# Transposing q with the DMA crossbar instead of TensorE, for batches 2 to 7 of an attention and mixture-of-experts kernel

## The chip, the cores and the metric

The kernel runs on one core of one Trainium2 chip. The metric is the device time of one execution in microseconds (us), the median of several runs. Runs of the kernel before spread over about 0.5%, so a difference under 3 us is read with care.

## The reference

Linear attention with cosine weights, whose output feeds a mixture of eight experts with balanced gates. Only the attention matters here:

```python
B, H, S, D = 8, 8, 576, 64

def phi(x, c, s):
    r = np.maximum(x, 0.0)
    return np.concatenate([r * c, r * s], axis=-1)      # 64 -> 128 features

q_p, k_p = phi(q, cos_w, sin_w), phi(k, cos_w, sin_w)
kv  = einsum('bhsf,bhsd->bhfd', k_p, v)
z   = sum(k_p, axis=2)
num = einsum('bhsf,bhfd->bhsd', q_p, kv)
den = einsum('bhsf,bhf->bhs', q_p, z)[..., None] + 1e-06
attn = num / den                                         # then gates and eight experts
```

## The kernel before

The kernel computes attention batch by batch, in blocks. Block `j` holds TensorE's feed-forward matmuls of the first expert for tokens that are ready, cut into 16 slots, and each slot also carries some attention work: batch `b = j + 1` is finished (denominators, division, product), batch `b + 1` is prepared, and batch `b + 2` is loaded. The heads go in four pairs, 0 to 3. Order matters a lot: instructions of TensorE, VectorE and ScalarE stay in written order, and the DMA issues of the SP engine form one queue that is worked off in order.

q has its sequence on the partitions; the products need the features there. So q must be transposed, nine 128x128 blocks a pair. The parts that the change touches (cuts marked `# ...`):

```python
def load(b, half, names="qkv", held_back=False):      # POOL's DMA queue, f32 -> f16
    for name in names:
        x = ld.tile([P, 2, C, D], F16, name=f"{name}_ld")
        # ... one 288 KB transfer for two head pairs

def prep_q(b, hk):
    q_p = qp_pool.tile([P, C, 2, D], F16, name="q_p")
    ve.tensor_tensor(out=q_p[:], in0=loaded.pop(("q", b, hk))..., in1=cs, op=ALU.mult)
    qps[b, hk] = q_p

def turn(b, hk, i, scalar=None):                       # three of the nine blocks
    if i == 0:
        qTs[b, hk] = qT_pool.tile([P, C, P], F16, name="q_pT")
    t_ps = ps_s.tile([P, 512], FP32, name="small_ps")
    for c in range(i * C3, (i + 1) * C3):
        te.matmul(out=t_ps[...], lhsT=qps[b, hk][:, c]..., rhs=ident[:], ...)
    # rectify on the way out of PSUM: se.activation(Relu) or ve.tensor_scalar(max 0)

def denominators(b):
    for h in range(H):                                 # pair 3 comes last
        for j in range(3):
            te.matmul(out=den_ps[...], lhsT=zsel[:, h, :], rhs=qTs[b, hk][...], ...)
    # ... ve: add eps, reciprocal -> den
    if b >= 3:
        r = dram.tile([96, C3 * HP], FP32, name="r")
        nc.sync.dma_start(out=r[:], in_=den[:])        # to DRAM
        for hk in range(HK):                           # and back, broadcast over partitions
            rb = rb_pool.tile([P, C * HP], FP32, name="rb")
            for hh in range(2):
                nc.sync.dma_start(out=rb[...], in_=r[...].to_broadcast(...))

def attend(b, hk):
    # num_ps = kv.T @ q_pT on TensorE, then on VectorE:
    ve.tensor_tensor(out=xT[...], in0=num_ps[i]..., in1=rb[...], op=ALU.mult)

# the schedule of a block j from 3 on, batch b = j + 1 (gates and one sums call cut;
# blocks 1 and 2 prepare pair 3 of their own batch in slot 0)
at(j, 0, sums, b, 1)
for i, (hk, k_) in enumerate(turns[8:]):               # last 4 of the 12 turns
    at(j, i, turn, b, hk, k_, k_ != 1)
at(j, 4, denominators, b)
for hk in range(HK):
    at(j, 12 + hk, attend, b, hk)
for slot, fn, hk in ((4, prep_k, 0), (5, prep_q, 0), (6, prep_kv, 0), (6, prep_k, 1),
        (7, prep_q, 1), (8, prep_kv, 1), (9, prep_k, 2), (10, prep_q, 2),
        (11, prep_kv, 2), (11, prep_k, 3), (13, prep_kv, 3), (15, prep_q, 3)):
    at(j, slot, fn, b + 1, hk)
for i, (hk, k_) in enumerate(turns[:8]):
    at(j, 8 + i, turn, b + 1, hk, k_, k_ != 1)
if 1 <= j and b + 2 < B:
    for half in range(2):
        at(j, 13 + 2 * half, load, b + 2, half, "qkv", True)
```

The softmax here doesn't subtract the row's maximum and nothing guards it: scores larger than these inputs give would overflow.

Of the kernel before, what the change touches and what calls it, by code (L numbers as in the profile page):

```python
# [11 lines left out]
F16 = mybir.dt.float16  # L12

AX = mybir.AxisListType
ALU = mybir.AluOpType
# [10 lines left out]
def kernel(  # L26
# [10 lines left out]
    nc = tc.nc  # L37
    P = nc.NUM_PARTITIONS

    B, H, S, D = q.shape  # L40
# [5 lines left out]
    C = S // HP  # L46
# [71 lines left out]
    te, ve, se = bound  # L118
# [62 lines left out]
    with ExitStack() as p1:  # L181
# [5 lines left out]
        qT_pool = p1.enter_context(tc.tile_pool(name="qT_pool", bufs=6))  # L187
# [6 lines left out]
        loaded = {}  # L194
        sources = {"q": q, "k": k, "v": v}

        def load(b, half, names="qkv", held_back=False):
# [28 lines left out]
            out=ident[:], in_=ones_sq[:], pattern=[[-1, P]], compare_op=ALU.is_equal,  # L226
# [13 lines left out]
        def keep_busy(n):  # L240
# [12 lines left out]
            out=wrap[:], in0=gidx[:], scalar1=float(S), scalar2=None, op0=ALU.is_ge  # L253
# [3 lines left out]
            out=sval[:], in0=wrap[:], scalar=-float(S), in1=gidx[:],  # L257
            op0=ALU.mult, op1=ALU.add,
# [20 lines left out]
        with nc.allow_low_precision("sums of zeros and ones"):  # L279
            ve.tensor_reduce(  # L280
                out=lo[:], in_=rows[:, :, 1, :], axis=AX.XY, op=ALU.add, negate=True
# [3 lines left out]
                out=sel[:], in0=rows[:, 0:3, 0, :], in1=rows[:, 0:3, 1, :], op=ALU.add  # L285
            )
        ve.tensor_copy(
            out=spread.rearrange("p j hk hh d -> p (j hk hh) d"),
            in_=sel[:].rearrange("p j h -> p (j h)").unsqueeze(2).to_broadcast([P, 3 * H, D]),
# [12 lines left out]
        kps, qps, qTs, kvs, hls, rbs = {}, {}, {}, {}, {}, {}  # L302
# [13 lines left out]

        def prep_q(b, hk):

            q_p = qp_pool.tile([P, C, 2, D], F16, name="q_p")
            ve.tensor_tensor(  # L320
                out=q_p[:], in0=loaded.pop(("q", b, hk)).unsqueeze(2).to_broadcast([P, C, 2, D]),
                in1=cs, op=ALU.mult,
            )
            qps[b, hk] = q_p

        def prep_kv(b, hk, copy=ve.tensor_copy):
            k16, v16 = (loaded.pop((name, b, hk)) for name in "kv")
# [9 lines left out]

        def turn(b, hk, i, scalar=None):

            if i == 0:  # L340
                qTs[b, hk] = qT_pool.tile([P, C, P], F16, name="q_pT")
            t_ps = ps_s.tile([P, 512], FP32, name="small_ps")
            for c in range(i * C3, (i + 1) * C3):
                te.matmul(
                    out=t_ps[:, (c - i * C3) * P : (c - i * C3 + 1) * P],
                    lhsT=qps[b, hk][:, c].rearrange("p a d -> p (a d)"),
                    rhs=ident[:],
                    start=True,
                    stop=True,
                )  # L350
            dst = qTs[b, hk][:, i * C3 : (i + 1) * C3, :].rearrange("p c s -> p (c s)")
            if (3 * hk + i) % 2 == 0 if scalar is None else scalar:
                se.activation(out=dst, in_=t_ps[:, 0 : C3 * P], func=AF.Relu)
            else:
                ve.tensor_scalar(
                    out=dst, in0=t_ps[:, 0 : C3 * P], scalar1=0.0, scalar2=None, op0=ALU.max
                )
# [160 lines left out]
        prep_pair(0, 1)  # L518
        sums_made(0, 0, begun[0])
        prep_q(0, 0)  # L520
        begun.append(sums_begun(0, 1))
        keep_busy(12)
        prep_q(0, 1)
        for hk in range(HK):
            for i in range(3):
                turn(0, hk, i, hk < 2 or i == 0)
            keep_busy(8)
            if hk == 0:
                sums_made(0, 1, begun[1])
            if hk < 2:  # L530
                prep_q(0, hk + 2)
# [9 lines left out]
        for hk in range(HK):  # L541
# [7 lines left out]
            for kt in ((), (0,), (1,), (2, 3))[hk]:  # L549
                for ft, h_ps in enumerate(first_ps):  # L550
                    te.matmul(
                        out=h_ps[:],
# [14 lines left out]
        for j in range(B):  # L567
            b = j + 1
            if j == 0:
# [6 lines left out]
                for hk in range(HK):  # L576
                    for i in range(3):
                        at(0, 7 + hk, turn, 1, hk, i)
                    if hk == 0:
                        at(0, 7, lambda: sums_made(1, 1, begun[3]))  # L580
                    if hk < 2:
                        at(0, 7 + hk, prep_q, 1, hk + 2)
# [4 lines left out]
            elif b < B:  # L587
                if j <= 2:
                    at(j, 0, prep_q, b, 3)
                    at(j, 1, prep_kv, b, 3)  # L590
                    at(j, 1, sums, b, 0)
                    at(j, 3, sums, b, 1)
                    for i, (hk, k_) in enumerate(turns[2:]):
                        at(j, i // 2, turn, b, hk, k_, k_ != 1)
                else:
                    at(j, 0, sums, b, 1)
                    for i, (hk, k_) in enumerate(turns[8:]):
                        at(j, i, turn, b, hk, k_, k_ != 1)
                at(j, 5 if j <= 2 else 4, denominators, b)
                for hk in range(HK):  # L600
                    at(j, 8 + 2 * hk if j == 1 else 12 + hk, attend, b, hk)
# [460 lines left out]
    for e in range(1, E):  # L1062
# [3 lines left out]
        for n in range(NU):  # L1066
# [28 lines left out]
            if e == 1 and n == 0:  # L1095
# [9 lines left out]
                ve = nc.vector  # L1105
# [8 lines left out]
    while stream:  # L1114
        _, pair, name = stream.pop(0)
# [32 lines left out]
```

## Time and profile before

| | before |
|---|---|
| median time | 1001.2 us (999.5 to 1001.7, 4 runs) |
| span of the profiled run | 999.2 us |
| TensorE busy | 978.4 us |
| attention of batches 3 to 7, issue of the first r to that of the last | 87.5 us, four blocks of 19.7, 21.7, 24.8 and 21.3 |
| rest of the span after the last r | 826.7 us |

First the page's busy times and, from its picture of 40 slices of 25 us, TensorE, its granted clock (tenths of full speed) and the mean busy share of the 16 DMA engines (PE is TensorE, PEld its weight loads, DVE VectorE, ACT ScalarE, POOL GpSimd):

```profile
PE 978.4 (98%) x8002; PEld 685.7 (69%) x8002; DVE 811.5 (81%) x1828; ACT 572.9 (57%) x1268; POOL 60.3 (6%) x82
...
PE   7999999989999999999999999999999999999997
...
PEclk8999999999999999999999999999999999999999
DMA  9907773733002331034013320043113400104535
```

TensorE looks like the only limit. But DMA is about seven tenths busy in slices 4 to 6, where the attention runs (75 to 150 us), and the chain of waits tells of a second limit. One block of that chain follows; the columns are start in us, length in us, and what the chain went through (L109 is a line of the kernel; h_ps are feed-forward matmuls, small_ps the attention's; "issue" is time in which the profile shows nothing that was waited for):

```profile
103.38 1.36 DVE den L109
104.74 0.02 issue
104.75 3.69 DMA r<-den
...
111.01 4.29 DMA rb<-r
...
115.43 0.57 DVE xT L109
...
118.99 0.95 PE small_ps L109 x39
119.94 0.86 PE h_ps L109 x4
...
123.89 0.80 PE small_ps L109 x24
```

The reciprocals of a batch leave for DRAM (r), come back as a broadcast (rb), VectorE multiplies them into xT, TensorE works on to the denominators of the next batch (the last line, 24 matmuls), and the loop starts again. TensorE fills its waits with feed-forward matmuls, so it is busy in nearly all of the loop.

The loads of q, k and v stand in slots 13 and 15, that is between the last rb and the next r. In the same block (start, length, engine, line, operation, tiles):

```profile
95.70 0.71 POOL L201 DMA_DIRECT2D q_ld<-in_q_dram  x1 [18.07 <-DVE acc_lo L109]
...
99.95 0.72 POOL L201 DMA_DIRECT2D v_ld<-in_v_dram  x1
```

Six loads are issued from 95.7 to 100.0 us, the last lands at 108.3 us. No critical transfer is issued on the SP queue from 91.8 us (the last rb) to 104.75 us (r), so the loads disturb only the end of this gap: r, which lands 1.58 us after its issue where no loads run (the last block), takes 3.4 to 3.9 us in three of the blocks.

### The profile page before, as it was taken

To read this page: it belongs to the slowest core of one execution; us is meant where nothing else is said; L and a number is where in the kernel's file an instruction comes from. 1 tells how busy PE (TensorE), PEld (TensorE's weight loads), DVE (VectorE), ACT (ScalarE), POOL (GpSimd) and SP (SyncE) were. 2 spreads that over 40 slices of the span, in tenths; PEclk is the share of its full clock that TensorE was granted. 3 is DMA by queue.
4 is the path that set the end of the run, shared out by engine and by line. 5 is a ranking of instruction groups with operands and counts; after the bars stand their busy time and mean duration, and the time that the engine had idled before them with its cause. 6 is when DMAs were issued, how large, how long until landed. Compare 5 with 4: busy or idle time off the path is not lost.

```text
span 999.2 us, 20494 instructions
## 1 busy us (share of the span) xinstructions
PE 978.4 (98%) x8002; PEld 685.7 (69%) x8002; DVE 811.5 (81%) x1828; ACT 572.9 (57%) x1268; POOL 60.3 (6%) x82
## 2 busy tenths in 40 slices
PE   7999999989999999999999999999999999999997
PEld 7555545446777777777777777777777777777775
DVE  5877556588989888888879878988789888988887
ACT  5677656357777555555555555555555555555551
POOL 6302210001000000000000000000000000000001
PEclk8999999999999999999999999999999999999999
DMA  9907773733002331034013320043113400104535
GB/s 171 200 3 139 145 137 72 155 67 83 32 26 54 62 67 47 25 82 75 25 48 67 62 53 24 27 89 67 40 34 66 91 25 25 48 25 107 134 85 127
DMA packets 60800, 72.74 MB, mean 73 GB/s; under 512 B 5568, under 2 KB 52640, under 8 KB 60704
## 3 DMA queue, kind: packets, MB, share of 16 engines
q0 software_dynamic: 27232, 30.94, 19.7%
q1 hardware_dynamic: 33232, 40.25, 14.9%
q8 instruction: 62, 1.02, 0.4%
q14 instruction: 34, 0.28, 0.1%
q10 hardware_dynamic: 240, 0.26, 0.1%
HBM read 89.01 MB, written 13.34 MB: 102 GB/s over the span
## 4 chain that ended last, share of the span: by engine, by line
issue 76%; PE 14%; DMA 4%; DVE 3%; POOL 2%; SPq 1%; ACT 0%; POOLq 0%; DVEq 0%; ACTq 0%
PE h_ps L109 5%; PE small_ps L109 4%; PE y_ps L109 3%; DMA rb<-r 2%; PE rows_ps L109 1%; DMA r<-den 1%; DVE den L109 1%; SPq L423 1%; DMA k_ld<-in_k_dram 1%; POOL w2e L133 0%; DVE xT L109 0%; PE copied_ps L109 0%; POOL w1e L127 0%; POOL acc_lo L978 0%; DVE P_tok L109 0%
## 5 line engine op out<-in xcount | busy, mean ns | idle before, releaser
L821 DVE SCALAR_TENSOR_TENSOR acc_lo<-rows_ps,P_tok,acc_lo 128x512 f32<-128x512 f32 (+1 forms) x322 | 203.1, 639 | 74.8 <-PE rows_ps L109 74.8
L109 PEld LDWEIGHTS <-H 128*128 128x128 f16 x2080 | 203.0, 98 | 83.1 <-issue 1.2
L757 ACT CAST u<-h_ps 128x384 f16<-128x384 f32 x288 | 137.5, 478 | 131.4 <-PE h_ps L109 131.4
L109 PEld LDWEIGHTS <-w1e 128*128 128x128 f16 x1632 | 155.9, 98 | 60.2 <-issue 5.2
L751 DVE CUSTOM_DVE_ANT_0 H<-p_ps,u 128x384 f16<-128x384 f32 x329 | 180.9, 550 | 6.7 <-PE p_ps L109 6.4
L109 PEld LDWEIGHTS <-hs 128*128 128x128 f16 x1500 | 146.5, 98 | 56.4 <-issue 0.3
L109 PE MATMUL h_ps<-S,w1e 128*128 128x384 f16 x672 | 164.1, 326 | 1.1 <-ACT u L109 0.9
L109 PE MATMUL p_ps<-xT,T 128*128 128x384 f16 x672 | 164.1, 326 | 0.3 <-DVE H L751 0.2
L109 PE MATMUL h_ps<-xT,w1e 128*128 128x384 f16 (+1 forms) x616 | 152.6, 350 | 0.5 <-DVE xT L109 0.5
L109 PE MATMUL rows_ps<-V,H 128*128 128x256 f16 x1000 | 150.0, 273 | 0.7 <-DVE acc_hi L821 0.7
L109 PE MATMUL rows_ps<-w2e,hs 128*128 128x256 f16 x1000 | 150.0, 273 | 0.0
L789 ACT ACTIVATE H<-h_ps 128x384 f16<-128x384 f32 x144 | 70.6, 490 | 95.1 <-PE h_ps L109 95.1
L109 PEld LDWEIGHTS <-T 128*128 128x128 f16 x1008 | 98.1, 98 | 29.5 <-issue 3.0
L109 PE MATMUL rows_ps<-w2e,H 128*128 128x256 f16 (+1 forms) x568 | 91.2, 285 | 0.0
L770 ACT COPY copied_ps<-h_ps 128x384 f32<-128x384 f32 x144 | 67.5, 469 | 35.2 <-PE h_ps L109 35.2
L780 ACT ACTIVATE H<-copied_ps 128x384 f16<-128x384 f32 x144 | 70.8, 492 | 20.4 <-PE copied_ps L109 20.4
L109 PE MATMUL copied_ps<-xT,w1e 128*128 128x384 f16 x336 | 82.1, 326 | 0.0
L109 PE MATMUL h_ps<-S,T 128*128 128x384 f16 x336 | 81.8, 325 | 0.3 <-ACT copied_ps L109 0.3
L109 PE MATMUL copied_ps<-w2e,H 128*128 128x256 f16 x504 | 75.5, 272 | 0.0
L109 PE MATMUL rows_ps<-V,hs 128*128 128x256 f16 x500 | 74.9, 272 | 0.0
L821 DVE SCALAR_TENSOR_TENSOR acc_lo<-copied_ps,P_tok,acc_lo 128x256 f32<-128x256 f32 x126 | 60.0, 476 | 0.4
L821 DVE SCALAR_TENSOR_TENSOR acc_hi<-rows_ps,P_tok,acc_hi 128x512 f32<-128x512 f32 (+1 forms) x56 | 41.3, 737 | 20.5 <-PE rows_ps L109 19.7
(126 smaller groups left out, 993.6 us busy)
## 6 DMA issues: line engine op xcount, KB each, us to landing
S<-x_saved SPq DMA_DIRECT2D x108, 192.0 KB, 2.4
out_dram<-acc_lo SPq DMA_DIRECT2D x62, 128.0 KB, 2.4
w1e<-in_moe_w_dram POOLq DMA_DIRECT2D x7, 1024.0 KB, 9.1
w2e<-in_moe_w_dram POOLq DMA_DIRECT2D x7, 1024.0 KB, 9.6
rb<-r SPq DMA_DIRECT2D x40, 144.0 KB, 4.3
k_ld<-in_k_dram POOLq DMA_DIRECT2D x16, 288.0 KB, 7.7
v_ld<-in_v_dram POOLq DMA_DIRECT2D x16, 288.0 KB, 8.4
q_ld<-in_q_dram POOLq DMA_DIRECT2D x16, 288.0 KB, 8.1
```

What stands on the lines that cost most here:

```text
L109: i = getattr(self.engine, name)(*args, **kwargs)
L423: nc.sync.dma_start(out=rb[hh * HP : (hh + 1) * HP, :].rearrange("p (j s) -> p j s", j=3), in_=r[:].rearrange("(j r) s -> r j s", r=32)[h ...
L751: latest = ve._custom_dve(TENSOR_ADD_SAT, out=out, in0=ps[:, 0:TU], in1=t[:], s0=FP32_MAX, s1=0.0)
L757: se.copy(out=t[:], in_=ps[:, 0:TU])
L770: se.copy(out=Y[:, 0:TU], in_=X[:, 0:TU])
L780: se.activation(out=h11, in_=Y[:, 0:TU], func=AF.Relu)
L789: se.activation(out=h12, in_=X[:, 0:TU], func=AF.Relu)
L821: ve.scalar_tensor_tensor(out=a, in0=rows, scalar=P_tok[:, g, self.e : self.e + 1], in1=a, op0=ALU.mult, op1=ALU.add,)
```

## The change

Its intent is to take work off the busiest engine. For batches 2 to 7 the 216 TensorE transposes and their 72 evictions from PSUM go. Instead VectorE rectifies q in place, multiplies it by the cosines as before, and one transposing DMA for each head pair writes `q_pT` directly. The transfer is issued on the SP queue, which also carries r and rb.

```diff
         def prep_q(b, hk):
 
+            q16 = loaded.pop(("q", b, hk))
+            by_dma = b >= 2
+            if by_dma:
+                ve.tensor_scalar(
+                    out=q16, in0=q16, scalar1=0.0, scalar2=None, op0=ALU.max
+                )
             q_p = qp_pool.tile([P, C, 2, D], F16, name="q_p")
             ve.tensor_tensor(
-                out=q_p[:], in0=loaded.pop(("q", b, hk)).unsqueeze(2).to_broadcast([P, C, 2, D]),
+                out=q_p[:], in0=q16.unsqueeze(2).to_broadcast([P, C, 2, D]),
                 in1=cs, op=ALU.mult,
             )
-            qps[b, hk] = q_p
+            if by_dma:
+                qTs[b, hk] = qT_pool.tile([P, C, P], F16, name="q_pT")
+                nc.sync.dma_start(
+                    out=qTs[b, hk][:], in_=q_p[:].rearrange("p c a d -> p (c a d)"),
+                    transpose=True,
+                )
+            else:
+                qps[b, hk] = q_p
...
         def turn(b, hk, i, scalar=None):
 
+            if b >= 2:
+                return
             if i == 0:
```

## The prediction

> What bounds the kernel now. TensorE is 98% busy over the 999 us span (busy shares). The change acts in the attention stage, from about 75 to 184 us for batches 2 to 7. There TensorE is 90 to 100% busy in each 25 us stretch (windows), so little idle is to be won. The chain of waits shows a second limit for batches 3 to 7, a loop of 21 to 25 us a block: denominator matmuls, reciprocal 1.36, r to DRAM 1.6 to 3.9, rb back 4.3 to 6.0, multiply into xT, TensorE to the next denominators. VectorE waits for rb 18.6 us in all. DMA is 0.78 busy at 140 GB/s from 75 to 150 us (windows).
>
> Removed. 216 TensorE transposes (6 batches x 4 pairs x 9). In the chain nine take 0.50 us, and four h_ps matmuls are spaced 1.03 us with three of them against 0.86 without: 0.055 us each, 12 us of TensorE, 2.0 a batch. Evictions: 48 on ScalarE (0.49 us each, 23 us) and 24 on VectorE (0.55 us, 13 us), off the critical engine.
>
> Added. 24 VectorE rectifications of 128x576 f16, estimated at 0.2 to 0.45 us from the f16 copy of the same shape (0.44): 5 to 11 us, about what VectorE saves. 24 transposing transfers of 288 KB on the SP queue, which also issues r and rb. A plain 192 KB load lands in 2.4 us, rb of 144 KB beside the loads in 4.3. The Trainium skill, "DMA: Bandwidth & Descriptors", section "Latency and other measured facts", gives 261 GB/s for a transpose in one kernel: 1.1 us of data, an estimate of 3 to 4 us to landing. "VectorE: DVE Perf Modes", section "The three transpose paths", gives 1309 ns for one 128x128 block: nine in series would be 12 us. No trace here shows one. I expect about 5 us beside the loads.
>
> Critical path. Pairs 0 to 2 have slack. Pair 3 has little: its q_p is written in a block's last slot (118.65 to 119.4 us in one block), the denominator matmuls that read it start at 123.8, 4.4 us later, and k, v, q loads are issued from 117.6. SP is in order: eight rb issues take 5.8 us, the transposes come behind them; with three q_p buffers, pair 3's product waits until pair 0's transpose has landed. So pair 3's transposed q comes 0 to 4 us late in five blocks, TensorE stands at the denominators, and r and rb start later. Against it, 1.3 us a block (two thirds of the 2.0) leaves the loop. At 3 us to landing the kernel gains 6 to 10 us; at 5 to 6 it breaks even or loses a few; at 12 it loses 40 and more.
>
> Predicted: 1004 us, 8 in 10 within 988 to 1045. Faster by over 2%: 0.04; within 2%: 0.60; slower: 0.36. A gain over 2% needs 20 us, more than the TensorE work removed.
>
> What would show it. Right: transposes land in 4 to 7 us; TensorE busy falls by about 12 us; a new wait of the denominator matmuls for the transfer into q_pT; den, r, rb still in the chain, with the transpose among them; the rest after the stage unchanged in length. Wrong: landings under 3.5 us and no wait at the denominators (then 990 to 994); or landings over 10 us, late loads of k and v, a chain mostly of DMA (then above 1040).
>
> What would make it wrong: the cost of a transfer on the chip, which no trace here has; SP's time to issue one, if several us; transposes slowing rb and the loads.

## The result, and the profile after

The changed kernel takes 1030.1 us (1030.0 to 1031.5, 4 runs) against 1001.2 us: a ratio of 1.0295, 95% interval 1.028 to 1.031, slower. A ratio here is always the mean time of one kernel's runs over that of the other's runs in the same rounds, so it is not quite the ratio of the medians. The result is correct.

| | before | after |
|---|---|---|
| median time | 1001.2 us | 1030.1 us |
| TensorE busy | 978.4 us | 973.4 us |
| issue of the first r | 85.0 us | 93.0 us |
| four blocks, r to r | 19.7, 21.7, 24.8, 21.3 us | 28.2, 29.5, 29.5, 20.8 us |
| rest of the span after the last r | 826.7 us | 827.4 us |

Of the 29.2 us that the span grew, 8.0 were lost before the first r (in batch 3) and 20.5 in the four blocks after it; the 827 us behind them are the same. The page's lines after:

```profile
PE 973.4 (95%) x7786; PEld 674.6 (66%) x7786; DVE 807.7 (79%) x1828; ACT 553.6 (54%) x1220; POOL 60.4 (6%) x82
...
PE   7996666998999999999999999999999999999997
...
PEclk8998888999999999999999999999999999999999
DMA  9938889572401341013310431134013320113535
```

TensorE is six tenths busy in slices 4 to 7 (of 25.7 us each), its granted clock is down to 8 there, and DMA is at 8 to 9. One block of the chain, the counterpart of the one before:

```profile
98.79 4.60 DMA rb<-r
...
104.71 0.56 DVE xT L109
...
106.36 0.42 PE h_ps L109 x2
106.79 12.10 DMA q_pT<-q_p
118.88 0.04 issue
118.93 0.51 PE small_ps L109 x6
119.44 3.03 PE h_ps L109 x8
```

A new piece of 12.10 us stands in the loop: the transfer of pair 3. TensorE had already done 18 of the 24 denominator matmuls and stood before the last six, which read pair 3. Here are these matmuls and the issues near them in the timeline (the number in brackets is TensorE's idle time, and what ended it):

```profile
104.36 0.72 POOL L201 DMA_DIRECT2D q_ld<-in_q_dram  x1 [25.60 <-DVE acc_lo L109]
...
109.85 0.68 PE L109 MATMUL small_ps<-q_pT,zsel 128*32 128x192 f16 x18
...
118.93 0.51 PE L109 MATMUL small_ps<-q_pT,zsel 128*32 128x192 f16 x6 [8.40 <-DMA q_pT<-q_p]
```

The wait comes four times (who waited for whom, from 60 to 215 us: total, times, longest):

```profile
PE small_ps L109 <- DMA q_pT<-q_p: 35.4, 4, 9.3
```

The 24 transposes land 3.2 to 13.7 us after their issue, median 4.7. Exactly four take more than 7 us: pair 3 of batches 3 to 6, with 13.7, 12.1, 13.2 and 12.8 us. They are issued at 77.0, 106.8, 135.2 and 165.1 us, and the loads of the batch that follows (4 to 7) at 74.5 to 78.0, 104.4 to 108.5, 132.7 to 136.8 and 162.6 to 166.7 us, at the same moments. Pair 3 of batch 7 has no loads beside it and lands in 3.2 us.

The first theory was therefore: pair 3's transfer shares the DMA engines with the loads and becomes late; TensorE's wait for it is the loss. Rivals were that pair 3 is late because it queues behind pairs 1 and 2, that the added VectorE work or the SP queue holds the stage up, and that the clock drop after each standstill adds to it. It had also to be explained why 12 us of removed TensorE work are nowhere to be seen.

For all runs the loop is cut into three parts: r's issue to the first rb's issue; from there to the end of the last product into xT of that batch; from there to the next r. These numbers are worked out from the start, end and landing times in each trace, as means of the four blocks in us. Without loads means that the loads of batches 4 to 7 were left out. Times are medians, the parts come from one profiled run each; that of e8 was its fastest (993.3 us).

| kernel | time, us | ratio to before | a block | r to rb | rb to xT | xT to next r |
|---|---|---|---|---|---|---|
| before | 1001.2 | 1 | 21.9 | 3.3 | 10.9 | 7.7 |
| changed | 1030.1 | 1.0295 | 27.0 | 2.4 | 10.7 | 13.9 |
| changed, without loads (e1) | 991.2 | 0.9911 | 19.5 | 2.4 | 10.2 | 7.0 |
| before, without loads (e2) | 995.9 | 0.9947 | 20.4 | 1.6 | 11.0 | 7.8 |
| pairs 0 to 2 by crossbar (e3) | 1005.7 | 1.0044 | 22.5 | 3.9 | 10.7 | 7.9 |
| no transposes at all (e8) | 995.9 | 0.9956 | 20.8 | 4.0 | 9.8 | 7.0 |
| before, loads earlier (e9) | 1024.4 | 1.0236 | 27.6 | 1.6 | 16.7 | 9.3 |
| pair 3 alone by crossbar (e11) | 1033.0 | 1.0317 | 28.3 | 1.8 | 12.9 | 13.7 |

### The profile page after: what moved, and what is told of

It reads as the page before. It is cut to its first block, busy times and chain, and to the rows that moved or that the text cites. A ratio compares the mean times of both kernels' runs of the same rounds, so it can differ in the third digit from the quotient of the medians.

```text
span 1028.4 us, 20076 instructions
## 1 busy us (share of the span) xinstructions
PE 973.4 (95%) x7786; PEld 674.6 (66%) x7786; DVE 807.7 (79%) x1828; ACT 553.6 (54%) x1220; POOL 60.4 (6%) x82
## 4 chain that ended last, share of the span: by engine, by line
PE 88%; DMA 7%; DVE 2%; ACT 1%; POOL 1%; issue 1%; SPq 0%; DVEq 0%; POOLq 0%; ACTq 0%
PE rows_ps L109 32%; PE h_ps L109 26%; PE copied_ps L109 11%; PE p_ps L109 11%; DMA q_pT<-q_p 5%; PE y_ps L109 4%; PE small_ps L109 3%; DMA rb<-r 1%; DMA v_ld<-in_v_dram 1%; DVE xT L109 0%; SPq L438 0%; DVE den L109 0%; DVE acc_hi L836 0%; POOL hs_last L851 0%; DVE P_tok L109 0%
## 5 line engine op out<-in xcount | busy, mean ns | idle before, releaser
L109 PEld LDWEIGHTS <-w1e 128*128 128x128 f16 x1632 | 157.7, 99 | 72.5 <-issue 15.9
L109 PE MATMUL h_ps<-xT,w1e 128*128 128x384 f16 (+1 forms) x616 | 157.7, 365 | 1.9 <-DVE xT L109 1.8
L795 ACT ACTIVATE H<-copied_ps 128x384 f16<-128x384 f32 x144 | 70.8, 492 | 20.4 <-PE copied_ps L109 20.4
L109 ACT ACTIVATE hT<-h_ps 128x512 f16<-128x512 f32 x54 | 32.1, 598 | 62.3 <-PE h_ps L109 62.1
## 6 DMA issues: line engine op xcount, KB each, us to landing
k_ld<-in_k_dram POOLq DMA_DIRECT2D x16, 288.0 KB, 10.8
v_ld<-in_v_dram POOLq DMA_DIRECT2D x16, 288.0 KB, 10.8
```

The lines of the kernel that those rows point to most:

```text
L109: i = getattr(self.engine, name)(*args, **kwargs)
L795: se.activation(out=h11, in_=Y[:, 0:TU], func=AF.Relu)
```

## The experiments

Twelve kernels ran, each beside the kernel before on the same chip.

### e1: the changed kernel without loads

A wrong result: batches 4 to 7 reuse the tiles of batches 2 and 3.

```diff
+            if b >= 4:
+                for name in names:
+                    for i in range(2):
+                        loaded[name, b, 2 * half + i] = kept[name, b % 2, 2 * half + i]
+                return
             for name in names:
                 x = ld.tile(...)
```

> The changed kernel without the q, k, v loads of batches 4 to 7 (wrong result on purpose: those batches reuse the tiles of batches 2 and 3). Theory (pair 3's transpose shares the DMA engines packet for packet with the loads issued in the same slots): all transposes land in under 6 us, the four waits of TensorE at the denominators (35.4 us in the changed kernel) fall under 4 us in all, time 983 to 992. Rival 1 (pair 3 queues behind pairs 1 and 2 in its own queue): landings and waits stay, time above 1020. Rival 2 (the added VectorE work or the SP queue holds the stage up): time stays above 1005.

Measured: 991.2 us, ratio 0.9911 (0.988 to 0.994). TensorE waits nowhere for a transfer into q_pT, and the slowest transfer lands in 6.3 us (a pair 1, issued at 131.4 us), just over what was written; pair 3 of batches 3 to 7 lands in 3.2 to 3.4 us. The changed kernel loses 39 us by the loads, so the loads are the cause of the loss, and neither the added VectorE work, nor the SP queue, nor queueing behind pairs 1 and 2: all three are in this run too. That it is the loads beside pair 3, and not loads in general, is what e2, e10 and e11 add.

How the engines share can be read from the DMA view of a short stretch (queue, kind: packets, MB, share of the 16 engines' time). First the changed kernel while pair 3 of batch 4 is under way beside loads, 108 to 118 us; q0 are the loads (1152 byte packets), q1 the transpose (256 byte packets):

```profile
q0 software_dynamic: 1492, 1.61, 94.4%
q1 hardware_dynamic: 1173, 0.29, 20.2%
...
q_pT<-q_p SPq DMA_TRANSPOSE x1, 12.1
```

Then the same transfer without loads (e1), 118.5 to 120.5 us:

```profile
q1 hardware_dynamic: 1154, 0.29, 75.4%
...
q_pT<-q_p SPq DMA_TRANSPOSE x1, 3.3
```

Alone, 0.29 MB pass in under 2 us, at about 210 GB/s while they last. Beside the loads the same packets need about 8 us (1492 packets of the loads and 1173 of the transpose's queue in the stretch). The trace's packet records split the 12.1 to 13.7 us of the four late transfers: the first packet passes 3.8 to 4.2 us after the issue (alone 1.2), and from the first to the last of the 1152 it takes 7.7 to 9.2 us (alone 1.5), in which 840 to 1030 load packets pass as well. The load packets are 4.5 times as big and, at a median of 0.107 us in the trace's packet records, six times as long as those of the transpose (0.018 us alone). So the transpose's share in bytes is small: 0.29 MB against 1.61. About seven of the nine to ten added microseconds are thus packets that pass side by side; why the first one comes almost 3 us later than alone was not tested. The Trainium skill states the rule on the page "DMA: Bandwidth & Descriptors", section "Queues, rings and completion order": each SDMA engine "round-robins between the queue rows it has work for, at *packet* granularity". The counts, near one to one, fit that rule. They don't prove it: the packed trace doesn't name the engine of a packet, and whether its records are what the page calls packets isn't shown.

### e2: the kernel before without loads

The same edit on the kernel before, as a control.

> Control: the kernel before without the same loads (wrong result on purpose). Both theories: the loads are hidden before the change, apart from some rb that lands sooner; time 993 to 1000. If it falls by over 10 us, then taking loads away speeds both kernels and the run before this one tells less.

Measured: 995.9 us, ratio 0.9947 (0.992 to 0.997), as expected. The loads cost the kernel before 5 us and the changed kernel 39. Without loads the change gains by the medians, 995.9 to 991.2 us, but only 4.6 of the 12 us of TensorE work that it removes (one of the four runs of e1, 996.0, was no faster than e2, so the size of the gain is uncertain). The reason is in the windows of both (stretch, its length, busy us of each engine with instructions, granted clock, DMA share, GB/s). One block of e2, then one of e1:

```profile
105.20:125.90 20.70, 20.70 (x240) 10.75 (x237) 14.35 (x31) 13.87 (x29) 0.00 (x0) 1.00 0.24 63
```

```profile
104.20:123.80 19.60, 18.96 (x204) 8.60 (x200) 13.39 (x31) 10.39 (x21) 0.00 (x0) 1.00 0.56 126
```

In e2 TensorE is busy all of the 20.7 us, and the chain of waits from 105 to 147 us goes through TensorE alone: it bounds the block. In e1 it has less to do and is idle 0.64 of 19.6 us, and the chain goes through rb (4.79 us in this block) and xT: now the loop bounds it. The first limit went down by 2 us and the second one stood 1 us below the first.

### e3: only pairs 0 to 2 by the crossbar

```diff
-            by_dma = b >= 2
+            by_dma = b >= 2 and hk < 3
...
-            if b >= 2:
+            if b >= 2 and hk < 3:
                 return
```

> Pairs 0 to 2 of batches 2 to 7 by the crossbar, pair 3 by TensorE as before; right result. Theory (only pair 3 is late): no wait for a transfer at the denominators, 162 of the 216 TensorE transposes gone, 8.9 us, time 989 to 996. Rival (transposing transfers as such slow the loads, r and rb): time 1003 or more, with longer waits for rb.

Measured: 1005.7 us, ratio 1.0044 (1.002 to 1.006). The wait for the transfer is gone, as the theory said, but the time missed its range by 10 us and fits the rival: 9 us less of TensorE's work end in a kernel 4 us slower. VectorE's wait for rb rose from 18.6 to 22.9 us in all. In the table the part r to rb grew from 3.3 to 3.9 us a block. In the first three blocks r lands 4.0, 4.6 and 4.3 us after its issue, where before it was 2.0, 3.7 and 3.9. So the crossbar costs time even if nobody waits for a transpose's data. The reading at the time was that the transposes make r and rb slower, and that anything that delays them counts in full. e8, below, speaks against the first half: with no transposes at all r lands in 3.1, 4.7, 4.3 and 3.9 us, r to rb is 4.0 us and VectorE waits 22.3 us for rb, as here. The slower r and the longer waits appear with TensorE relieved, crossbar or not. What the run leaves standing is that the theory was too narrow: with pair 3 on TensorE the change still doesn't gain.

### e4: pair 3 prepared earlier

```diff
-        kp_pool = ...(name="kp_pool", bufs=4)
+        kp_pool = ...(name="kp_pool", bufs=3)
-        qT_pool = ...(name="qT_pool", bufs=6)
+        qT_pool = ...(name="qT_pool", bufs=7)
-                    (11, prep_kv, 2), (11, prep_k, 3), (13, prep_kv, 3), (15, prep_q, 3),
+                    (11, prep_q, 3), (11, prep_kv, 2), (11, prep_k, 3), (13, prep_kv, 3),
```

> All pairs by the crossbar, but pair 3's q is prepared in slot 11 and not 15 of a block from batch 4 on, with one more q_pT buffer (paid for by one k_p buffer less), so that its transfer starts before the loads; loads unmoved; right result. Theory: the transfer lands in under 7 us in batches 4 to 6, those three waits under 1 us, the wait of batch 3 (prepared in the earlier block form) stays at about 9 us: time 995 to 1003 with that one wait left. Rival 1 (own queue): pair 3 still lands 10 us or more after its issue, time above 1012.

Measured: 1019.4 us, ratio 1.0191 (1.016 to 1.022): a miss. The transfer did not start early enough, because the SP queue first issues eight rb. In the trace pair 3 is issued at 79.1, 107.0, 133.1 and 161.2 us, and the first load of the pair of loads at 76.5, 106.9, 132.5 and 161.8. Only in the last case did the transfer start before the loads, and there it landed in 5.4 us, without a wait; the others took 13.8, 9.8 and 14.3 us, and TensorE waited three times, 21.4 us in all (the first of them, batch 3, is prepared in block 2, which the edit leaves as it was). In that last block it was r that came late, 5.0 us after its issue. The order of transfer and loads decides, which is what the theory says; the edit was too weak to use it.

### e5: idle matmuls against the drop of the clock

```diff
+            if 3 <= b <= 6:
+                for _ in range(66):
+                    te.matmul(
+                        out=den_ps[:, 192:512], lhsT=ident[:], rhs=xT[:, 0, 0:320],
+                        start=True, stop=True,
+                    )
             for h in range(H):          # the denominators
```

> The changed kernel with 66 idle matmuls of 320 columns (8.8 us at full clock) put in front of the denominators of batches 3 to 6, where TensorE otherwise stands still for about 9 us; right result. Theory (each standstill also drops TensorE to half clock for some microseconds after it, about 8 us in all by the clock records): granted clock in the stage near 1.0, matmuls after the wait 0.22 us apart and not 0.46, time 1020 to 1026. Rival (the clock costs nothing on the chain): 1028 to 1034.

Measured: 1029.0 us, ratio 1.0276 (1.025 to 1.030), which overlaps the changed kernel's 1.0295. The clock in the stage is back at 1.00 (0.80 to 0.91 in the changed kernel), four matmuls of h_ps after the wait take 0.95 us and not 1.5 or more, and TensorE's wait is 1.0 us in all. No time is gained beyond the scatter. Theory and expectation fell: the half clock after a standstill is real, but TensorE has slack at that point, since what follows in the loop is r and rb: from the landing of pair 3 to the next r it is 2.2 to 2.5 us with the filler and 2.4 without. Filling an idle engine that waits for something else wins nothing.

### e6: transposes that nobody reads

```diff
# ... one tile `unused` added, one k_p buffer less
             qps[b, hk] = q_p
+            if b >= 2:
+                nc.sync.dma_start(
+                    out=unused[:], in_=q_p[:].rearrange("p c a d -> p (c a d)"),
+                    transpose=True,
+                )
```

> The kernel before, TensorE transposes kept, with the 24 crossbar transfers issued too, into a tile that nothing reads (one k_p buffer less to make room); right result. Nobody waits for a transfer's data. Theory (the change loses its time by TensorE's wait for pair 3): pair 3's transfers still take over 10 us in the four blocks with loads, but the time is only 1003 to 1012, what r, rb and the loads lose to the transfers. Rival (contention with r, rb and the loads is the main loss): 1015 to 1030.

Measured: 1022.8 us, ratio 1.022 (1.020 to 1.024), in the rival's range. But the experiment is flawed, so nothing is concluded from it for the split. All transfers write the same tile, so each waits on the SP queue for the one before it to land, and r stands behind them. The waits of the SP queue show it:

```profile
SPq L327 <- DMA unused<-q_p: 69.9, 19, 11.2
```

In one block the reciprocals were ready at 109.1 us and r was issued at 117.1. It shows another way to lose: in a queue that issues in order, a transfer that waits for its buffer holds up the critical transfer behind it.

### e7: no loads, and pair 0 behind rb

The SP queue of the changed kernel holds r, the transpose of pair 0, eight rb, then pairs 1 to 3. Here pair 0 was put behind the rb by an ordering edge, on top of e1.

```diff
-                        nc.sync.dma_start(out=rb[...], ...)
+                        last_rb[0] = nc.sync.dma_start(out=rb[...], ...)
...
-                nc.sync.dma_start(out=qTs[b, hk][:], ..., transpose=True)
+                not_before(last_rb[0], nc.sync.dma_start(out=qTs[b, hk][:], ..., transpose=True))
```

> The changed kernel without the loads of batches 4 to 7, as in the first experiment (wrong result on purpose), and pair 0's transpose put behind the eight rb issues on the SP queue and not between r and rb. Theory (without loads the loop den, r, rb, xT bounds a block, and the transpose's issue in it costs 0.8 us a block): first rb issue 1.6 us after r and not 2.4, time 2 to 4 us under the first experiment's 991.2. Rival (TensorE bounds it): 990 to 992.

Measured: 990.1 us, ratio 0.9886 (0.986 to 0.991), against e1's 0.9911 (0.988 to 0.994). The intervals overlap, and the run doesn't decide. r to rb did shrink from 2.4 to 1.6 us a block as foreseen, but rb to xT grew from 10.2 to 10.8, and the block came to 19.4 us instead of 19.5.

### e8: no transposes at all

A wrong result: batches 2 to 7 reuse batch 1's transposed q; no engine transposes, the loads run as before.

```diff
             qps[b, hk] = q_p
+            if b >= 2:
+                qTs[b, hk] = qTs[1, hk]
...
         def turn(b, hk, i, scalar=None):
+            if b >= 2:
+                return
```

> The kernel before with the transposes of batches 2 to 7 left out on every engine, with their evictions; those batches reuse batch 1's transposed q (wrong result on purpose). The upper bound of what freeing TensorE can give, 12 us of its work. Theory (the loop den, r, rb, xT bounds batches 3 to 7 beside TensorE): time 994 to 999. Rival (TensorE alone bounds the stage): 987 to 991.

Measured: 995.9 us, ratio 0.9956 (0.993 to 0.999), as expected. This is the most that this change could have won in this schedule had the crossbar been free: 5 us (1.5 to 7 by the interval), not 12. With TensorE relieved, VectorE's wait for rb grew from 18.6 to:

```profile
DVE xT L109 <- DMA rb<-r: 22.3, 10, 6.8
```

### e9: the kernel before with the loads earlier

After e3 the loads' tail, which meets r, looked like the thing to move.

```diff
-                    at(j, 13 + 2 * half, load, b + 2, half, "qkv", True)
+                    at(j, 8 + 2 * half, load, b + 2, half, "qkv", True)
```

> The kernel before with the q, k, v loads of batches 4 to 7 issued from slots 8 and 10 of a block and not 13 and 15; right result. Control for the next run, and a test of the loop alone: the loads' tail no longer meets r. Theory: r lands 1.6 us after its issue and not 3.4 to 3.9, rb loses up to 2 us; time 995 to 1001. Rival (r is slow for another reason, or rb loses all that r gains): 1001 or more.

Measured: 1024.4 us, ratio 1.0236 (1.022 to 1.025): a clear miss. r did land in 1.6 us in all blocks. But now the loads run beside rb, and rb lost far more than 2 us. One piece of the chain:

```profile
95.36 10.15 DMA rb<-r
```

It took 4.29 us in the kernel before. VectorE waits for rb 33.7 us in place of 18.6, and the part rb to xT is 16.7 us a block in place of 10.9. This kernel has no crossbar transposes at all, and loses 24 us with its urgent transfers beside the loads: from 96 to 105 us 942 packets of the SP queue passed beside 1207 of the loads. So what the change ran into is not special to the crossbar: in this kernel a transfer of the loop loses much when it runs beside all six loads. In slots 13 to 15 of the kernel before lay the one stretch of the loop in which the SP queue carried nothing urgent, and the loads had been put there. The change put an urgent transfer into it.

### e10: pairs 0 to 2 by the crossbar, loads earlier

The edits of e3 and e9 together.

> Pairs 0 to 2 by the crossbar, pair 3 by TensorE, with the loads issued from slots 8 and 10; right result. Theory (the transposes of pairs 0 to 2 cost time only by pushing r, rb and the loads): r back to 1.6 us, time 993 to 1000 against 1005.7 with the loads in slots 13 and 15. Rival (the crossbar transfers fill the DMA engines wherever they stand): 1004 or more.

Measured: 1030.4 us, ratio 1.0296 (1.028 to 1.031), a miss for the reason of e9. r is back at 1.6 to 1.7 us, rb to xT is 15.9 us a block. It doesn't tell whether the crossbar transfers fill the engines wherever they stand, since e9 alone accounts for most of it. But the trace tests the first theory once more: with the loads moved, it is now pairs 1 and 2 of batches 3 to 6 that are late, 8.2 to 15.8 us from issue to landing against 3.2 to 6.6 in e3, while in batch 7, without loads, they land in 4.0 and 4.6 us. What makes a transpose late is the company, whichever pair it is.

### e11: pair 3 alone by the crossbar

The reverse of e3 (`hk == 3` in both conditions).

> The reverse of the run with pairs 0 to 2: pair 3 of batches 2 to 7 by the crossbar, pairs 0 to 2 by TensorE, loads in slots 13 and 15 as before; right result. Theory (pair 3 is the one that costs): its transfer still takes 10 us or more in the four blocks with loads, TensorE waits 25 to 40 us at the denominators, time 1022 to 1034. Rival (the queueing of four transfers behind each other makes pair 3 late): landing under 7 us, time 1000 to 1010.

Measured: 1033.0 us, ratio 1.0317 (1.030 to 1.033). Six transfers in place of 24, and the whole loss (the interval overlaps that of the changed kernel, 1.028 to 1.031). The four beside loads land in 12.5, 12.8, 12.2 and 11.6 us with no transpose before them in the queue, the two others in 3.3 and 3.5. TensorE's waits:

```profile
PE small_ps L109 <- DMA q_pT<-q_p: 30.1, 4, 8.5
```

With e3 this splits the change: pair 3 carries the loss. Pairs 0 to 2 alone cost about 4 us net; the two don't add up to the change (32 and 4 us against 29), so they are not independent.

### e12: batch 7 alone by the crossbar

The one batch of 3 to 7 with no loads beside its transposes, pair 0 behind rb as in e7 (`b == 7` in both conditions). It was meant as the version that might beat both kernels.

> Only batch 7 by the crossbar, the one batch of 3 to 7 beside whose transposes no q, k, v loads run, with its pair 0 put behind the rb issues on the SP queue; batches 2 to 6 by TensorE; right result. Theory (without loads beside it the crossbar costs no wait and frees 2 us of TensorE, of which the loop lets about 1 through): no wait for the transfers, landing 3 to 6 us, time 0.5 to 2 us under the kernel before. Rival (the crossbar costs time even without loads): 2 us or more over it.

Measured: 1000.4 us against 1000.4 us, ratio 1.0002 (0.999 to 1.002). No wait for a transfer, landings of 3.9 to 5.2 us: no cost of the crossbar shows there, within the interval of about 1.5 us either way. Nor did the gain show; 0.5 us lies inside the interval, 2 us doesn't. No correct version tried here beats the kernel before.

## Why the prediction was right or wrong

The time, 1030.1 us, lies inside the stated range of 988 to 1045, but 26 us from the middle value (1004), and slower, the class that came, had been given 0.36 against 0.60 for within 2%. The place and the kind of the loss were foreseen; its size was not. That the time still fell inside the range is owed to the range's width, which is luck: for the landing that it expected, about 5 us, the prediction itself says that the kernel breaks even or loses a few. Point by point:

- "Pair 3 has little [slack]" and "TensorE stands at the denominators": right. The wait is there, at the last six of the 24 matmuls, with the loads issued beside it. e1, e10 and e11 show that it is pair 3 and the loads.
- "I expect about 5 us beside the loads", "0 to 4 us late": this is the step that failed. The median over all transfers is 4.7 us, but the four that count took 12.1 to 13.7 us and made TensorE wait 35.4 us in all, 8.9 each. The estimate took the bandwidth of a lone transfer (261 GB/s on the page "DMA: Bandwidth & Descriptors" of the Trainium skill; alone the trace shows about 210) and added a little for company. Counting packets would have come nearer, as an estimate made afterwards: the kernel before already showed load packets of 0.107 us. 1152 packets of a transpose over 16 engines are 72 an engine, and 72 turns behind such a packet are 7.7 us, plus the transfer's own 3.2 us: 11 us. The packets did take 7.7 to 9.2 us, but the estimate lacks the later first packet.
- "12 us" as the value of a landing time, with a loss of "40 and more": the mapping overshot. At 12 us and more the loss was 29.
- "In five blocks": four. Batch 7 has no loads beside it.
- "1.3 us a block leaves the loop": somewhat too high. A block shrinks by 1.1 us from the kernel before to e8, which puts all that removing the transposes could win at 5 us, and by 0.9 us from e2 to e1, where TensorE then stops being the limit. So "at 3 us to landing the kernel gains 6 to 10 us" was too high as well: in e1, with pair 3 at 3.2 to 3.4 us, the gain over e2 was 4.6.
- "TensorE busy falls by about 12 us": the page shows 5.0, but matmuls at half clock count longer there. Without loads and with the clock up in this stage (e1) busy time is 967.1 us, 11.3 less than before and 9.1 less than its own control e2 (976.2).
- VectorE's rectifications, estimated at 0.2 to 0.45 us: right, a median of 0.30 us, and they do not appear in the chain of the changed kernel in this stage (in other variants a few do, at 0.1 to 0.25 us each).
- "nine in series would be 12 us": refuted for this cause. A transfer of nine blocks alone lands in 3.2 us. The long landings come from company.
- "transposes slowing rb and the loads", named as a risk: seen for the loads. k loads land 10.8 us after issue in place of 7.7. For r and rb it isn't shown: r is as slow in e8, without any transpose, as in e3. Its share isn't isolated, since e6 was flawed.
- "The rest after the stage unchanged": right, 827.4 against 826.7 us.

The ledger, from r to r: pair 3's late transfer adds 6.2 us to the part from xT to the next r (7.7 to 13.9 a block), while r to rb falls by 0.9, because the loads are through when r at last goes out. In e1, with pair 3 landing in 3.2 us, that same part is 7.0.

What stays open is in part where the 10 us between e3 (1005.7) and e8 (995.9) come from. The two traces are 11.5 us apart. r to rb is no slower in e3 (3.9 against 4.0 us a block). 3.8 us are lost before the first r, in batches 2 and 3, where e3 shows 3.4 us at half clock from 53.8 us and e8 none. In the four blocks xT to next r is 0.9 longer in e3 (0.5 in three of them, which is what pair 3's nine TensorE transposes take) and rb to xT 0.9 longer. Which transfer, or which added VectorE work, causes the rest isn't shown.

## What to carry to other kernels

Before moving work from a full engine to DMA, ask which transfers are in a loop that something waits for, and what else the DMA engines carry at that very moment; a share of 0.78 over a stage says less than whether loads are issued in the same slot. As a first estimate, cost a transfer beside others by its number of packets times the length of the neighbour's packet, not by its bytes over a bandwidth; here this gave 11 us where 12 to 14 came, and it was fitted to this one case. And find the upper bound first by leaving the work out altogether: here that one run (about 5 us at best) would have argued against the change before it was built.

## What the Trainium skill lacked or had wrong

- "DMA: Bandwidth & Descriptors", section "Latency and other measured facts": it gives a transpose's bandwidth (261 GB/s) but nothing for a transpose beside loads. Here 288 KB land in 3.2 us alone and in 12 to 14 us beside loads of 1152 byte packets, with near one packet of each queue for one of the other (1173 against 1492 in 10 us). The page speaks of 256-byte tiles and rows of a transpose, but not of what the trace shows: 288 KB are 1152 packets, which take 7.7 to 9.2 us beside longer ones and 1.5 us alone.
- The same page, section "DMA Transpose (X-bar)": it gives no time for the issue; elsewhere the page has only cycle counts of "previous generations" in a comparison with trn3. On the SP queue one took 1.25 to 2.5 us (median 1.4) against 0.6 us for an rb broadcast, and issues behind it wait.
- "VectorE: DVE Perf Modes", section "The three transpose paths": it compares 1309 ns (crossbar) with 390 ns (TensorE) for one 128x128 block. In this kernel a TensorE block in a row of nine costs 0.055 us of TensorE (without the eviction from PSUM), and nine blocks in one crossbar transfer land in 3.2 us, 0.36 us a block. This doesn't refute the page, which speaks of one block, but as costs for blocks in bulk both numbers are far too high.
